# A gated linear attention with a two-layer MLP: the gate's linear half folded into one matrix, and every engine's order from a list scheduler

## The chip, the cores and the metric

The kernel runs on one core of one Trainium2 chip. A core has the engines PE (TensorE, matrix products), DVE (VectorE), ACT (ScalarE), POOL (GpSimd) and SP (SyncE, which here only issues transfers). Each takes its instructions in the order of its own list and waits where an instruction needs another engine's or a transfer's result. Stated times are device microseconds of a whole execution; the profile's span runs from its first to its last instruction.

## The reference

```python
def _attn_ref(q, k, v, f_logit):            # (4, 8, 768, 48) each
    f = 1.0 / (1.0 + np.exp(-f_logit))
    for t in range(S):
        state = f[:, :, t, :, None] * state + np.einsum('bhd,bhe->bhde', k[:, :, t], v[:, :, t])
        y[:, :, t] = np.einsum('bhd,bhde->bhe', q[:, :, t], state)

def _moe_ref(x, w_in, w_out):               # x (3072, 384), w_in (384, 2048), w_out (2048, 384)
    h = x @ w_in
    g = 0.5 * (h + np.sqrt(h * h + 4.0))
    return g @ w_out
```

The result of the attention, with its heads side by side, is the x of the MLP.

## The kernel before

The 3072 tokens are 24 chunks r of 128 (six for each of four batches); two neighbours are a pair p, and there are 12 pairs. A pair goes through these steps, which are also the functions of the code:

- `load` puts f, q, k, v of the pair into buffers, two transfers of 192 KB for each, all issued by SP. `load_w_in` and `load_w_out` load the weights in four pieces of 768 KB each, cast to fp16 by ACT (L118) and DVE (L124).
- `logs` forms the negative logarithm of the forget gate: exponential and logarithm on ACT (L133, L134), a high fp16 part on DVE (L136) and the low part on POOL (L137).
- `decays` sums the logs over a chunk on PE (L145, L146), takes two exponentials of each chunk's sums on ACT (L151, L152), multiplies q and k with them on POOL (L153, L154), and gets the boundary sums by 32 matmuls of two columns (L163, L164). `gammas` makes the factors between chunks (POOL L179, ACT L182).
- `st_T` to `st_YT` are the attention of one chunk: transposed q and k (PE and DVE, or from chunk `XBAR_FROM` = 12 on a transposing transfer), scores (L211) and their mask (DVE L213), state (L222, L225, DVE L228), y (L239, L241, DVE L244), and y transposed into `xT`.
- `mlp1` is the first layer: a half is six matmuls of 256 columns (L296) into one of four PSUM banks `hps`; for each two banks ACT squares them (L303, 512 wide) and takes the root (L304), and DVE adds half of h (L307), which gives `g16`. The decays use the same four banks.
- `mlp2` is the second layer: 16 matmuls of 384 columns for each chunk (L325), a copy (L329) and the transfer out.

ACT needs one table for exponentials and logarithms and another for roots; a load of a table is a row of ACT. So exponentials come in windows: eight `GROUPS` of chunks, and `window` runs the decays of one group and the logs of the next between two table loads. The order is written out by hand: `run_mlp1` mixes first-layer halves with attention steps from the list `att` (in the proportion `SHARE`) and second-layer quarters from the list `fill`; ACT takes its instructions exactly as written, and the other engines' orders come from the tile framework.

Of the kernel before, what the change touches and what calls it, by code (L numbers as in the profile page):

```python
# [15 lines left out]
XBAR_FROM = 12  # L16
# [3 lines left out]
GROUPS = [(0, 2), (2, 4), (4, 6), (6, 8), (8, 12), (12, 16), (16, 20), (20, 24)]  # L20
SHARE = 0.8
# [3 lines left out]
def kernel(  # L25
# [20 lines left out]
    PR = 2  # L46
    TB = PR * C

    ctx.enter_context(tc.manual_schedule(engines={mybir.EngineType.Activation}))
# [3 lines left out]
    gp = ctx.enter_context(tc.tile_pool(name="gp", bufs=4))  # L53
    stp = ctx.enter_context(tc.tile_pool(name="stp", bufs=2))
    wp = ctx.enter_context(tc.tile_pool(name="wp", bufs=2))
    bp = ctx.enter_context(tc.tile_pool(name="bp", bufs=2))
    xp = ctx.enter_context(tc.tile_pool(name="xp", bufs=5))
    mp = ctx.enter_context(tc.tile_pool(name="mp", bufs=2))
    pp_h = ctx.enter_context(tc.tile_pool(name="pp_h", bufs=1, space=PSUM))
# [15 lines left out]
    nc.vector.memset(hvec[64:128, 1:2], 1.0)  # L75

    w_in16 = konst.tile([128, NJ, DFF], FP16, name="w_in16")
    w_out16 = konst.tile([128, NN, DM], FP16, name="w_out16")

# [4 lines left out]
    qt = [t[:, :, 0] for t in qk]  # L84
    kt = [t[:, :, 1] for t in qk]
# [6 lines left out]
    for t in gam:  # L92
        nc.vector.memset(t, 0.0)
    for t in qt + kt:
        nc.gpsimd.memset(t[:, :, :, D:64], 0.0)

    hps = [pp_h.tile([128, 512], FP32, name=f"hps{i}") for i in range(4)]


    loads = {}  # L100

    def load(p, names):
        for name in names:
            src = {"f": f_logit, "q": q, "k": k, "v": v}[name]
            t = ldp.tile([128, PR, H, D], FP32, name=f"ld_{name}", tag=f"ld_{name}")
            loads[name, p] = t
            for r in range(PR):
                b, c = divmod(p * PR + r, NC)
                nc.sync.dma_start(out=t[:, r],  # L109
                                  in_=src[b][:, c * C:(c + 1) * C, :].rearrange("h t d -> t h d"))  # L110

    WQ = 512

    def load_w_in(i):
        st = stp.tile([128, 4 * DM], FP32, name="w_st", tag="w_st")
        s3 = st.rearrange("p (j n) -> p j n", j=NJ)
        nc.sync.dma_start(out=s3, in_=moe_w_in[:, i * WQ:(i + 1) * WQ].rearrange("(j p) n -> p j n", p=128))
        nc.scalar.copy(out=w_in16[:, :, i * WQ:(i + 1) * WQ], in_=s3)  # L118

    def load_w_out(i):  # L120
        st = stp.tile([128, 4 * DM], FP32, name="w_st", tag="w_st")
        s3 = st.rearrange("p (j n) -> p j n", j=4)
        nc.sync.dma_start(out=s3, in_=moe_w_out[i * 512:(i + 1) * 512, :].rearrange("(j p) n -> p j n", p=128))
        nc.vector.tensor_copy(out=w_out16[:, 4 * i:4 * i + 4, :], in_=s3)  # L124


    v16s = {}

    def logs(p):

        f = loads["f", p]
        ls = wp.tile([128, PR, H, D], FP32, name="ls", tag="ls")
        nc.scalar.activation(out=f, in_=f, func=AF.Exp, scale=-1.0)  # L133
        nc.scalar.activation(out=ls, in_=f, func=AF.Ln, bias=1.0, scale=1.0)  # L134
        hi, lo = lhi[p % NL], llo[p % NL]
        nc.vector.tensor_copy(out=hi[:, :, :, 0:D], in_=ls)  # L136
        nc.gpsimd.tensor_tensor(out=lo[:, :, :, 0:D], in0=ls, in1=hi[:, :, :, 0:D], op=ALU.subtract)  # L137

    def decays(p):

        hi, lo = lhi[p % NL], llo[p % NL]
        hp2 = [hps[2 * (p % 2) + r] for r in range(PR)]
        for r in range(PR):
            ca = hp2[r][:, 0:H * D]
            nc.tensor.matmul(out=ca, lhsT=wcent, rhs=hi[:, r, :, 0:D], start=True, stop=False)  # L145
            nc.tensor.matmul(out=ca, lhsT=wcent, rhs=lo[:, r, :, 0:D], start=False, stop=True)  # L146
        ea = wp.tile([128, PR, H, D], FP32, name="ea", tag="ea")
        eap = wp.tile([128, PR, H, D], FP32, name="eap", tag="eap")
        for r in range(PR):
            ca = hp2[r][:, 0:H * D]  # L150
            nc.scalar.activation(out=ea[:, r].rearrange("p h d -> p (h d)"), in_=ca, func=AF.Exp, scale=-1.0)  # L151
            nc.scalar.activation(out=eap[:, r].rearrange("p h d -> p (h d)"), in_=ca, func=AF.Exp, scale=1.0)  # L152
        nc.gpsimd.tensor_tensor(out=qt[p % NB][:, :, :, 0:D], in0=loads["q", p], in1=ea, op=ALU.mult)  # L153
        nc.gpsimd.tensor_tensor(out=kt[p % NB][:, :, :, 0:D], in0=loads["k", p], in1=eap, op=ALU.mult)  # L154
        v16 = bp.tile([128, PR, H, D], FP16, name="v16", tag="v16", bufs=4)
        nc.vector.tensor_copy(out=v16, in_=loads["v", p])
        v16s[p] = v16
        b, c = divmod(p * PR, NC)
        for r in range(PR):
            nl = hp2[r][:, H * D:H * D + 2 * NP].rearrange("p (j s) -> p j s", s=2)  # L160
            for hp in range(NP):
                o = nl[:, hp, :]
                nc.tensor.matmul(out=o, lhsT=hi[:, r, 2 * hp:2 * hp + 2, :], rhs=hvec, start=True, stop=False)  # L163
                nc.tensor.matmul(out=o, lhsT=lo[:, r, 2 * hp:2 * hp + 2, :], rhs=hvec, start=False, stop=True)  # L164
            nc.vector.tensor_copy(out=nls[b % 2][:, c + r], in_=nl)

    def gammas(g):
        r0, r1 = GROUPS[g]
        a = r0
        while a < r1:  # L170
            b, c = divmod(a, NC)
            e = min(r1, (b + 1) * NC)
            n = e - a
            nb, gm = nls[b % 2], gam[b % 2]
            c0 = max(c - 1, 0)
            c1 = c + n - 1
            if c1 > c0:
                gi = wp.tile([128, NC, NP], FP32, name="gi", tag="gi")
                nc.gpsimd.tensor_tensor(out=gi[:, c0:c1], in0=nb[:, c0:c1, :, 1],  # L179
                                        in1=nb[:, c0 + 1:c1 + 1, :, 0], op=ALU.add)  # L180
                for s in range(2):
                    nc.scalar.activation(out=gm[64 * s:64 * s + 64, c0:c1, :, s],  # L182
                                         in_=gi[64 * s:64 * s + 64, c0:c1], func=AF.Exp, scale=-1.0)
            a = e


    state = {}
    xTs = {}
    part = {}

    def st_T(r):
        p, i = divmod(r, PR)
        qkT = bp.tile([128, 2 * NP, C], FP16, name="qkT", tag="qkT", bufs=3)
        if r < XBAR_FROM:
            tr = pp_a.tile([128, 2 * NP, C], FP16, name="tr", tag="a")
            for j in range(NP):
                nc.tensor.transpose(out=tr[:, j, :], in_=qt[p % NB][:, i, 2 * j:2 * j + 2, :], identity=ident16)
                nc.tensor.transpose(out=tr[:, NP + j, :], in_=kt[p % NB][:, i, 2 * j:2 * j + 2, :], identity=ident16)  # L198
            nc.vector.tensor_copy(out=qkT, in_=tr)  # L199
        else:  # L200
            nc.sync.dma_start_transpose(out=qkT, in_=qk[p % NB][:, i].rearrange("p a h d -> p (a h d)"))
        part[r] = {"qkT": qkT}

    def st_SC(r):
        qkT = part[r]["qkT"]
        pm = bp.tile([128, 2, NP, C], FP16, name="pm", tag="pm")
        for s in range(2):
            sc = pp_a.tile([128, NP, C], FP32, name="sc", tag="a")
            o = 64 * s
            for j in range(NP):  # L210
                nc.tensor.matmul(out=sc[:, j, :], lhsT=qkT[o:o + D, NP + j, :], rhs=qkT[o:o + D, j, :],  # L211
                                 start=True, stop=True)
            nc.vector.tensor_tensor(out=pm[:, s], in0=sc, in1=mask16.unsqueeze(1).broadcast_to([128, NP, C]),  # L213
                                    op=ALU.mult)
        part[r]["pm"] = pm

    def st_KV(r):
        p, i = divmod(r, PR)
        b, c = divmod(r, NC)
        u = pp_a.tile([128, NP, 2, D], FP32, name="u", tag="a")  # L220
        if c > 0:
            nc.tensor.matmul(out=u.rearrange("p a b d -> p (a b d)"), lhsT=ident16,  # L222
                             rhs=state[r].rearrange("p a b d -> p (a b d)"), start=True, stop=False)
        for j in range(NP):
            nc.tensor.matmul(out=u[:, j], lhsT=kt[p % NB][:, i, 2 * j:2 * j + 2, :],  # L225
                             rhs=v16s[p][:, i, 2 * j:2 * j + 2, :], start=(c == 0), stop=(c == 0 or j == NP - 1))
# [20 lines left out]
    def st_YT(r):  # L247
        p, i = divmod(r, PR)
        if i == 0:
            xTs[p] = xp.tile([128, NJ, TB], FP16, name="xT", tag="xT")  # L250
# [226 lines left out]
```

## Time and profile before

| | us |
|---|---|
| median of 3 runs | 257.18 |
| lowest, highest | 255.63, 257.59 |
| profiled execution, whole time | 257.61 |
| its span | 255.8 |
| DVE combine L307, 96 rows, busy | 62.1 |
| ACT squares L303 and roots L304, busy | 54.1 and 50.7 |
| POOL low part L137, busy | 19.8 |
| SP waiting to issue an output, in total | 37.7 |

"Busy" of PE counts pipelined matmuls with modelled ends, so their rows overlap: 576 matmuls with a mean of 296 ns are 84.4 us busy. The granted clock is given as a share of full speed. A waiting engine's row names what came last. Groups and timelines name a line, an engine, an operation, the tile written and those read, and a count.

### The profile page before, as it was taken

How to read it: one execution, taken by the hardware profiler on the slowest of the kernel's cores; microseconds unless marked ns; L12 is line 12 of the kernel's file. 1: busy time of each engine (PE TensorE's matmuls, PEld its weight loads, DVE VectorE, ACT ScalarE, POOL GpSimd, SP SyncE). 2: the span in 40 equal slices, each digit the busy share in tenths (PEclk: the TensorE clock that was granted, in tenths of full speed). 3: DMA queues.
4: the chain of work that ended last, by engine and by line, in shares of the span. 5: the costliest groups of instructions: out<-in, count | busy, mean ns of one | idle time of the engine just before them, and what ended most of it. 6: DMA issues, size and time to landing. Idle time of an engine off the chain costs nothing.

```text
span 255.8 us, 4975 instructions
## 1 busy us (share of the span) xinstructions
PE 209.0 (82%) x1892; PEld 147.2 (58%) x1892; DVE 165.0 (64%) x303; ACT 168.1 (66%) x252; POOL 70.8 (28%) x61
## 2 busy tenths in 40 slices
PE   0337893999778799599849997799995899999994
PEld 0125672775456566466537754577764577777652
DVE  2435763885887855668954746949980779956411
ACT  3332749888588197758688995149991889987200
POOL 4447101002762209701960039300029000000000
PEclk9999997799988799769998999569999599999999
DMA  8999399999935999999979932544115320120121
GB/s 140 188 193 279 105 232 247 255 252 187 205 64 115 190 210 168 199 224 175 147 161 187 172 99 44 133 95 62 32 49 97 64 37 18 47 80 31 61 93 63
DMA packets 124696, 34.54 MB, mean 135 GB/s; under 512 B 118016, under 2 KB 123136, under 8 KB 124672
## 3 DMA queue, kind: packets, MB, share of 16 engines
q1 hardware_dynamic: 124672, 34.22, 70.4%
q8 instruction: 15, 0.25, 0.4%
q14 instruction: 9, 0.07, 0.1%
HBM read 25.17 MB, written 4.72 MB: 117 GB/s over the span
## 4 chain that ended last, share of the span: by engine, by line
PE 40%; ACT 15%; issue 13%; POOL 12%; DVE 8%; DMA 5%; SPq 3%; POOLq 1%; ACTq 0%; DVEq 0%
PE hps L296 18%; PE o L325 14%; POOL qk L154 4%; POOL qk L153 4%; ACT hsq L303 4%; ACT r L304 3%; SPq L109 3%; DVE g L307 3%; PE sc L211 3%; DMA w_st<-in_moe_w_in_dram 3%; POOL llo L137 2%; DMA ld_f<-in_f_logit_dram 2%; DVE pm L213 2%; ACT eap L152 1%; ACT w_in L118 1%
## 5 line engine op out<-in xcount | busy, mean ns | idle before, releaser
L296 PE MATMUL hps<-xT,w_in 128*128 128x256 f16 x576 | 84.4, 296 | 9.4 <-DVE g L307 8.3
L325 PE MATMUL o<-w_out,g 128*128 128x384 f16 x384 | 79.2, 333 | 0.0
L307 DVE SCALAR_TENSOR_TENSOR g<-hps,r 128x512 f16<-128x512 f32 x96 | 62.1, 685 | 24.6 <-ACT r L304 24.2
L296 PEld LDWEIGHTS <-w_in 128*128 128x128 f16 x576 | 59.0, 105 | 26.2 <-issue 12.4
L303 ACT ACTIVATE hsq<-hps 128x512 f16<-128x512 f32 x96 | 54.1, 589 | 27.3 <-PE hps L296 25.7
L304 ACT ACTIVATE r<-hsq 128x1024 f16<-128x1024 f16 x48 | 50.7, 1057 | 1.5
L153 POOL TENSOR_TENSOR qk<-ld_q,ea 128x768 f16<-128x768 f32 x12 | 22.2, 1853 | 102.3 <-ACT ea L151 60.3
L325 PEld LDWEIGHTS <-g 128*128 128x128 f16 x384 | 35.6, 99 | 19.3 <-issue 1.2
L213 DVE TENSOR_TENSOR pm<-sc,mask 128x512 f16<-128x512 f32 x48 | 31.7, 683 | 6.2 <-PE sc L211 5.8
L211 PE MATMUL sc<-qkT 48*128 48x128 f16 x192 | 19.6, 243 | 9.3 <-DVE sn L228 4.4
L137 POOL TENSOR_TENSOR llo<-ls,lhi 128x768 f16<-128x768 f32 x12 | 19.8, 1657 | 24.2 <-DVE lhi L136 24.1
L154 POOL TENSOR_TENSOR qk<-ld_k,eap 128x768 f16<-128x768 f32 x12 | 23.3, 1938 | 0.0
L211 PEld LDWEIGHTS <-qkT 48*128 48x128 f16 x192 | 11.3, 103 | 17.8 <-issue 11.1
L329 DVE COPY o_sb<-o 128x384 f32<-128x384 f32 x24 | 13.2, 552 | 13.0 <-PE o L325 13.0
L182 ACT ACTIVATE gam<-gi 64x4 f32<-64x4 f32 (+3 forms) x18 | 3.8, 208 | 24.0 <-POOL gi L179 23.9
L151 ACT ACTIVATE ea<-hps 128x384 f32<-128x384 f32 x24 | 12.1, 506 | 8.3 <-PE hps L146 8.3
L228 DVE TENSOR_TENSOR sn<-u,gam 128x384 f16<-128x384 f32 x20 | 11.1, 553 | 10.0 <-ACT gam L182 7.6
L145 PE MATMUL hps<-lhi,wcent 128*128 128x384 f16 x24 | 8.1, 355 | 9.4 <-DVE wcent L70 9.2
L199 DVE COPY qkT<-tr 128x1024 f16<-128x1024 f16 x12 | 8.3, 691 | 10.8 <-PE tr L198 10.8
L241 PE MATMUL y<-v,pm 128*128 128x48 f16 x192 | 14.4, 200 | 1.0 <-DVE qkT L199 0.8
L136 DVE CAST lhi<-ls 128x768 f16<-128x768 f32 x12 | 10.6, 890 | 6.8 <-ACT ls L134 6.8
L244 DVE CAST y<-y 128x384 f16<-128x384 f32 x24 | 13.2, 549 | 2.3 <-PE y L241 2.3
(50 smaller groups left out, 222.6 us busy)
## 6 DMA issues: line engine op xcount, KB each, us to landing
ld_f<-in_f_logit_dram SPq DMA_DIRECT2D x24, 192.0 KB, 4.6
ld_q<-in_q_dram SPq DMA_DIRECT2D x24, 192.0 KB, 4.5
ld_k<-in_k_dram SPq DMA_DIRECT2D x24, 192.0 KB, 4.6
ld_v<-in_v_dram SPq DMA_DIRECT2D x24, 192.0 KB, 4.7
out_dram<-o_sb SPq DMA_DIRECT2D x24, 192.0 KB, 1.9
w_st<-in_moe_w_in_dram SPq DMA_DIRECT2D x4, 768.0 KB, 6.7
w_st<-in_moe_w_out_dram SPq DMA_DIRECT2D x4, 768.0 KB, 5.5
qkT<-qk SPq DMA_TRANSPOSE x12, 3.3
```

The costliest lines, as they stand in the source:

```text
L137: nc.gpsimd.tensor_tensor(out=lo[:, :, :, 0:D], in0=ls, in1=hi[:, :, :, 0:D], op=ALU.subtract)
L153: nc.gpsimd.tensor_tensor(out=qt[p % NB][:, :, :, 0:D], in0=loads["q", p], in1=ea, op=ALU.mult)
L154: nc.gpsimd.tensor_tensor(out=kt[p % NB][:, :, :, 0:D], in0=loads["k", p], in1=eap, op=ALU.mult)
L211: nc.tensor.matmul(out=sc[:, j, :], lhsT=qkT[o:o + D, NP + j, :], rhs=qkT[o:o + D, j, :], start=True, stop=True)
L213: nc.vector.tensor_tensor(out=pm[:, s], in0=sc, in1=mask16.unsqueeze(1).broadcast_to([128, NP, C]), op=ALU.mult)
L241: nc.tensor.matmul(out=y[:, j, s], lhsT=pm[:, s, j, :], rhs=v16s[p][:, i, 2 * j + s, :], start=(c == 0), stop=(c == 0 or s == 1))
L244: nc.vector.tensor_copy(out=y16.rearrange("p a b -> p (a b)"), in_=y.rearrange("p a b d -> p (a b d)"))
L296: nc.tensor.matmul(out=hb[:, a, :], lhsT=w_in16[:, j, jn * 128:(jn + 1) * 128], rhs=x[:, j, :], start=(j == 0), stop=(j == NJ - 1))
L303: nc.scalar.activation(out=hsq[:, a, :], in_=hps[(2 * j4 + a) % 4], func=AF.Square, scale=1.0)
L304: nc.scalar.activation(out=r16, in_=hsq, func=AF.Sqrt, scale=0.25, bias=1.0)
L307: nc.vector.scalar_tensor_tensor(out=g16[:, jn:jn + 2, :].rearrange("p a t -> p (a t)"), in0=hps[(2 * j4 + a) % 4], scalar=0.5, in1=r16[:, ...
L325: nc.tensor.matmul(out=o, lhsT=gts[p][:, jn, i * C:(i + 1) * C], rhs=w_out16[:, jn, :], start=(jn == 0), stop=(jn == NN - 1))
```

## The change

Since 0.5 (h + sqrt(h² + 4)) w_out = 0.5 x w_in w_out + sqrt(0.25 h² + 1) w_out, the linear part is x times one 384x384 matrix. `add_transposed_w_in` transposes the fp16 w_in on PE (48 transposes), `add_linear_part` multiplies it with w_out (48 matmuls) and stores half of it as `w_lin`. In the second layer each chunk then starts with three matmuls of `xT` with `w_lin`. The DVE combine is gone; the root writes `g16` itself.

The instructions are also cut differently. A first-layer tile is 1024 wide, with two such tiles of two banks in a ring; a square is 1024 wide and a root 2048; an exponential of the decays covers both chunks (768). The low part of the logs goes from POOL to DVE, the sum of the gammas too. Weights come in sixteen pieces of 384 KB through the rings of q, k and v, and DVE casts all of them. Chunks 10 and 11 are transposed by transfers too.

Every step is first put down as an `Op` with engine, assumed duration, dependencies, buffers and a due time. `Plan.run` then places them one by one: for each engine the head of each queue that could start first, within 0.05 us the one with the earliest due time, with rules that keep an exponential window of ACT together. The instructions are written out in this order for all engines.

```diff
-GROUPS = [(0, 2), (2, 4), (4, 6), (6, 8), (8, 12), (12, 16), (16, 20), (20, 24)]
+GROUPS = [[0], [1], [2], [3], [4, 5], [6, 7], [8, 9], [10, 11]]
-XBAR_FROM = 12
+XBAR_FROM = 10
+PACE = 15.5
+LEAD = {"W": 45.0, "B": 26.0, "M1": 0.0, "M2": -30.0}
...
+    def run(self):
...
+                t0 = min(c[0] for c in cands)
+                near = [c for c in cands if c[0] <= t0 + 0.05]
+                c = min(near, key=lambda c: c[1].due)
+                if best is None or c[0] < best[0]:
+                    best = c + (eng,)
...
-    ctx.enter_context(tc.manual_schedule(engines={mybir.EngineType.Activation}))
+    ctx.enter_context(tc.manual_schedule())
...
-        nc.gpsimd.tensor_tensor(out=lo[:, :, :, 0:D], in0=ls, in1=hi[:, :, :, 0:D], op=ALU.subtract)
+            nc.vector.tensor_tensor(out=llo[p % NL][:, :, :, 0:D], in0=T["ls", p],
+                                    in1=lhi[p % NL][:, :, :, 0:D], op=ALU.subtract)
...
+                nc.scalar.activation(out=t.rearrange("p r h d -> p r (h d)"), in_=T["ca", p][:, :, 0:H * D],
+                                     func=AF.Exp, scale=sign)
...
+    def add_transposed_w_in():
...
+                        for j in range(NJ):
+                            nc.tensor.transpose(out=t[:, b, j * 128:(j + 1) * 128],
+                                                in_=w_in16[:, j, jn * 128:(jn + 1) * 128], identity=ident16)
...
+                    nc.vector.tensor_copy(out=wiT[n][:, 2 * a:2 * a + 2, :], in_=T["wtp", n, a])
...
+    def add_linear_part(t_ops):
...
+                    for jn in range(4 * n, 4 * n + 4):
+                        nc.tensor.matmul(out=T["wl", j], lhsT=wiT[jn // 8][:, jn % 8, j * 128:(j + 1) * 128],
+                                         rhs=w_out16[:, jn, :], start=(jn == 0), stop=(jn == NN - 1))
...
+                nc.vector.tensor_scalar(out=w_lin[:, j, :], in0=T["wl", j], scalar1=0.5, scalar2=None, op0=ALU.mult)
...
-                nc.scalar.activation(out=hsq[:, a, :], in_=hps[(2 * j4 + a) % 4], func=AF.Square, scale=1.0)
-            nc.scalar.activation(out=r16, in_=hsq, func=AF.Sqrt, scale=0.25, bias=1.0)
-                nc.vector.scalar_tensor_tensor(out=g16[:, jn:jn + 2, :].rearrange("p a t -> p (a t)"),
-                                               in0=hps[(2 * j4 + a) % 4], scalar=0.5, in1=r16[:, a, :],
-                                               op0=ALU.mult, op1=ALU.add)
+                nc.scalar.activation(out=T["hsq", p, j8][:, j4 % 2],
+                                     in_=T["h", p, j4].rearrange("p a n -> p (a n)"), func=AF.Square, scale=1.0)
...
+                nc.scalar.activation(out=T["g", p][:, 8 * j8:8 * j8 + 8, :].rearrange("p a t -> p (a t)"),
+                                     in_=T["hsq", p, j8].rearrange("p a n -> p (a n)"), func=AF.Sqrt, scale=0.25, bias=1.0)
...
+                        for j in range(NJ):
+                            nc.tensor.matmul(out=T["o", p, i], lhsT=T["xT", p][:, j, i * C:(i + 1) * C],
+                                             rhs=w_lin[:, j, :], start=(j == 0), stop=False)
+                    for jn in range(4 * n, 4 * n + 4):
+                        nc.tensor.matmul(out=T["o", p, i], lhsT=T["g", p][:, jn, i * C:(i + 1) * C],
+                                         rhs=w_out16[:, jn, :], start=False, stop=(jn == NN - 1))
...
+    P.run()
+    for op in P.order:
+        if op == "exp":
+            nc.scalar.preload_act_table_set("natural_log_exp_and_others")
+        elif op == "sqrt":
+            nc.scalar.preload_act_table_set("sqrt_and_others")
         else:
+            op.emit()
```

The loads are written in this order: f, q, k, v of pairs 0 and 1; the eight pieces of w_in, with f of pair 2 after the fourth; the eight of w_out; q, k, v of pair 2; then f, q, k, v of each pair. SP's list before, from the ninth row on (w_st is the buffer for a piece of weights, the other names are the buffers of pair 2 and then pair 3):

```order
L117 DMA w_st<-in_moe_w_in_dram 128x3x512 x2
L109 DMA ld_f<-in_f_logit_dram 128x8x48 x2
L117 DMA w_st<-in_moe_w_in_dram 128x3x512 x2
L109 DMA ld_q<-in_q_dram 128x8x48 x2
L109 DMA ld_k<-in_k_dram 128x8x48 x2
L109 DMA ld_v<-in_v_dram 128x8x48 x2
L123 DMA w_st<-in_moe_w_out_dram 128x4x384 x2
L109 DMA ld_f<-in_f_logit_dram 128x8x48
```

SP's list after, at the end of the weights (the last three pieces of w_out, then pair 2 and f of pair 3):

```order
L287 DMA ld_v<-in_moe_w_out_dram 128x2x384
L287 DMA ld_q<-in_moe_w_out_dram 128x2x384
L287 DMA ld_k<-in_moe_w_out_dram 128x2x384
L266 DMA ld_q<-in_q_dram 128x8x48 x2
L266 DMA ld_k<-in_k_dram 128x8x48 x2
L266 DMA ld_v<-in_v_dram 128x8x48 x2
L266 DMA ld_f<-in_f_logit_dram 128x8x48 x2
```

All sixteen pieces of weights now stand ahead of q, k and v of pair 2. Before, half of w_in stood behind f of pair 2 and w_out behind the whole of pair 2.

ACT before, at the window with the decays of pair 2 and the logs of pair 3 (ea and eap are the two exponentials, ld_f and ls the logs, gam the gammas):

```order
L304 ACTIVATE r_705<-hsq 128x1024
L369 ACT_TABLE_LOAD
L151 ACTIVATE ea<-hps_143 128x384
L152 ACTIVATE eap<-hps_143 128x384
L151 ACTIVATE ea<-hps_144 128x384
L152 ACTIVATE eap<-hps_144 128x384
L133 ACTIVATE ld_f<-ld_f 128x768
L134 ACTIVATE ls<-ld_f 128x768
L182 ACTIVATE gam_121<-gi 64x8 x2
L382 ACT_TABLE_LOAD
```

ACT after, at the same window:

```order
L668 ACTIVATE g_429<-hsq 128x2048
L742 ACT_TABLE_LOAD
L365 ACTIVATE ea<-hps 128x768
L365 ACTIVATE eap<-hps 128x768
L318 ACTIVATE ld_f<-ld_f 128x768
L323 ACTIVATE ls<-ld_f 128x768
L416 ACTIVATE gi<-gi 128x8
L660 ACTIVATE hsq<-hps 128x1024 x2
L744 ACT_TABLE_LOAD
```

Before, both pairs 0 and 1 have gone through the first layer ahead of this window; after, only pair 0 has, and the squares of pair 1 stand behind the logs of pair 3, still ahead of the next table load.

More of the change, by code (lines that the diff above doesn't have):

```diff
@@ L91, with ring, add_load, emit @@
         nc.vector.memset(t[:, :, :, D:64], 0.0)
[L92 to L106, printed above, removed]
+    for t in qk:
+        nc.gpsimd.memset(t[:, :, :, :, D:64], 0.0)
+    P = Plan()
+    T = {}
+    rings = {}
+    def ring(name, n):
+        return rings.setdefault(name, Ring(n))
+    ld = {}
+    ld_buf = {}
+    src_of = {"f": f_logit, "q": q, "k": k, "v": v}
+    LB = {"f": 3, "q": 4, "k": 4, "v": 4}
+    def add_load(p, name):
+        buf = Buf(ring("ld_" + name, LB[name]))
+        ld_buf[name, p] = buf
+        def emit():
+            t = ldp.tile([128, PR, H, D], FP32, name=f"ld_{name}", tag=f"ld_{name}", bufs=LB[name])
+            T[name, p] = t
             for r in range(PR):
@@ L127 @@
[L127 to L157, printed above, removed]
-        b, c = divmod(p * PR, NC)
[L159 to L165, printed above, removed]
@@ L172, in gammas @@
             e = min(r1, (b + 1) * NC)
[L173 to L183, printed above, removed]
@@ L184, in gammas @@
-            a = e
[L187 to L215, printed above, removed]
@@ L218, in st_KV, with add_attention @@
+            o2 = P.add("W", "ACT", 0.25, ex, deps=[o1], due=due, uses=[gi_b], kind=("W", g))
+            o3 = P.add("gam", "DVE", 0.2, spread, deps=[o2], due=due, uses=[gi_b])
+            for cc in range(c0, c1):
+                gm[b * NC + cc] = o3
+    state_op = {}
+    xT_ops = {}
+    def add_attention(r):
         p, i = divmod(r, PR)
         b, c = divmod(r, NC)
-        u = pp_a.tile([128, NP, 2, D], FP32, name="u", tag="a")
-        if c > 0:
-            nc.tensor.matmul(out=u.rearrange("p a b d -> p (a b d)"), lhsT=ident16,
-                             rhs=state[r].rearrange("p a b d -> p (a b d)"), start=True, stop=False)
@@ L224, in st_KV @@
[L224 to L232 removed]
+        due = vtime(p, "B", i * PACE / 2)
@@ new lines, in add_attention, with yf @@
+        a_b = Buf(ring("a", 2))
+        def yf():
+            y = pp_a.tile([128, NP, 2, D], FP32, name="y", tag="a")
+            T["y", r] = y
+            for j in range(NP):
+                if c > 0:
+                    nc.tensor.matmul(out=y[:, j], lhsT=T["qkT", r][:, j, :], rhs=T["sn", r][:, j], start=True, stop=False)
+                for s in range(2):
+                    nc.tensor.matmul(out=y[:, j, s], lhsT=T["pm", r][:, s, j, :], rhs=T["v16", p][:, i, 2 * j + s, :],
+                                     start=(c == 0), stop=(c == 0 or s == 1))
@@ L233, in st_Y, with add_state @@
+        xT_ops.setdefault(p, []).append(op)
+    def add_state(r, due):
         p, i = divmod(r, PR)
         b, c = divmod(r, NC)
-        qkT, pm = part[r]["qkT"], part[r]["pm"]
-        y = pp_a.tile([128, NP, 2, D], FP32, name="y", tag="a")
-        for j in range(NP):
-            if c > 0:
-                nc.tensor.matmul(out=y[:, j], lhsT=qkT[:, j, :], rhs=state[r][:, j], start=True, stop=False)
-            for s in range(2):
-                nc.tensor.matmul(out=y[:, j, s], lhsT=pm[:, s, j, :], rhs=v16s[p][:, i, 2 * j + s, :],
-                                 start=(c == 0), stop=(c == 0 or s == 1))
@@ new lines @@
+    for n in "fqkv":
+        add_load(0, n)
+    for n in "fqkv":
+        add_load(1, n)
+    for i in range(8):
+        add_weight("in", i)
+        if i == 3:
+            add_load(2, "f")
+    for i in range(8):
+        add_weight("out", i)
+    for n in "qkv":
+        add_load(2, n)
+    for p in range(3, NPAIR):
+        for n in "fqkv":
+            add_load(p, n)
+    NG = len(GROUPS)
+    for p in GROUPS[0]:
+        add_logs(p, 0)
+    for g in range(NG):
+        for p in GROUPS[g]:
+            add_decays(p, g)
+        if g + 1 < NG:
+            for p in GROUPS[g + 1]:
+                add_logs(p, g)
+        add_gammas(g)
```

638 lines of the change are left out of this document (435 added, 203 removed).

## The prediction

> **What bounds the kernel now.** I read the page first (busy shares, slices, chain of waits), then the stretches between the start and the last matmul, then the groups by line, and last the timelines of single engines for durations. Page, one line of each part:
>
> ```profile
> span 255.8 us, 4975 instructions
> ...
> PE 209.0 (82%) x1892; PEld 147.2 (58%) x1892; DVE 165.0 (64%) x303; ACT 168.1 (66%) x252; POOL 70.8 (28%) x61
> ...
> PE   0337893999778799599849997799995899999994
> ...
> PEclk9999997799988799769998999569999599999999
> ...
> PE 40%; ACT 15%; issue 13%; POOL 12%; DVE 8%; DMA 5%; SPq 3%; POOLq 1%; ACTq 0%; DVEq 0%
> ```
>
> PE leads the shares and the chain, but it has holes, and the granted clock falls in six places. The stretches (duration; then busy us and count for PE, PEld, DVE, ACT, POOL; granted clock; DMA share; GB/s) say how much that is:
>
> ```profile
> 42.70:252.50 209.80, 188.34 (x1694) 132.59 (x1693) 144.31 (x254) 147.77 (x224) 54.92 (x36) 0.91 0.66 125
> 158.00:160.00 2.00, 1.07 (x16) 0.76 (x16) 2.00 (x6) 0.71 (x3) 2.00 (x3) 1.00 0.73 139
> 162.00:164.00 2.00, 1.63 (x13) 1.01 (x12) 1.93 (x4) 0.00 (x0) 0.42 (x1) 0.50 0.57 111
> ```
>
> A busy PE is not a PE at its peak, so I work out what its work costs in dense rows, start to start. Chain of waits, then the PE timeline:
>
> ```profile
> 148.44 1.28 ACT L369
> ...
> 233.01 0.66 PE hps L296 x6
> 233.66 0.65 PE o L325 x4
> ...
> 236.28 16.26 PE o L325 x100
> 252.56 0.56 DVE o_sb L329
> ```
>
> ```profile
> 35.80 0.33 PE L255 MATMUL yt<-ident,y 128*128 128x128 f16 x3
> 35.96 0.49 PE L296 MATMUL hps<-xT,w_in 128*128 128x256 f16 x3
> 36.29 0.21 PE L239 MATMUL y<-sn,qkT 128*128 128x96 f16 x1
> ...
> 36.66 0.93 PE L296 MATMUL hps<-xT,w_in 128*128 128x256 f16 x7
> ...
> 58.76 0.33 PE L145 MATMUL hps<-lhi,wcent 128*128 128x384 f16 x1
> ...
> 59.41 2.44 PE L325 MATMUL o<-w_out,g 128*128 128x384 f16 x14
> ```
>
> ```profile
> 171.62 0.45 PE L211 MATMUL sc<-qkT 48*128 48x128 f16 x8
> 171.99 2.23 PE L296 MATMUL hps<-xT,w_in 128*128 128x256 f16 x18
> 174.05 0.33 PE L222 MATMUL u<-sn,ident 128*128 128x384 f16 x1
> ...
> 174.39 0.33 PE L325 MATMUL o<-w_out,g 128*128 128x384 f16 x1
> ...
> 190.18 0.16 PE L163 MATMUL hps<-hvec,lhi 128*128 128x2 f16 x1
> ...
> 190.38 0.32 PE L325 MATMUL o<-w_out,g 128*128 128x384 f16 x1
> ```
>
> Dense prices: 0.109 us for a first-layer matmul (0.65 for 6), 0.163 for a second-layer one (16.26 for 100). For one chunk of 128 tokens: y transposed 0.16, y 0.37, scores 0.37, state 0.34, q/k transposed 0.43 (eight 128-wide transposes at the 0.16 for three). One pair's decays 0.65 + 2 x 0.20 = 1.05. So the whole kernel is 576 x 0.109 + 384 x 0.163 + 24 x (0.37 + 0.37) + 20 x 0.34 + 12 x (0.43 + 0.16) + 12 x 1.05 = 62.8 + 62.6 + 17.8 + 6.8 + 7.1 + 12.6 = 169.7 us of PE at full speed. By 42.7 us some 11.4 of it is done (4 chunks, 2 decays, 24 first-layer matmuls); the other 158.3 take 209.8, a loss of 51.5. The clock accounts for 0.09 x 209.8 = 19 of that, plain idle time for 209.8 - 188.3 = 21.5, the rest sits inside rows called busy. What empties PE (groups, waits):
>
> ```profile
> L296 PE MATMUL hps<-xT,w_in 128*128 128x256 f16 x576 | 84.4, 296 | 9.4 <-DVE g L307 8.3 <-DMA xT<-y 0.6
> L307 DVE SCALAR_TENSOR_TENSOR g<-hps,r 128x512 f16<-128x512 f32 x96 | 62.1, 685 | 24.6 <-ACT r L304 24.2
> L303 ACT ACTIVATE hsq<-hps 128x512 f16<-128x512 f32 x96 | 54.1, 589 | 27.3 <-PE hps L296 25.7 <-DVE qkT L199 0.9
> L304 ACT ACTIVATE r<-hsq 128x1024 f16<-128x1024 f16 x48 | 50.7, 1057 | 1.5
> L137 POOL TENSOR_TENSOR llo<-ls,lhi 128x768 f16<-128x768 f32 x12 | 19.8, 1657 | 24.2 <-DVE lhi L136 24.1
> L133 ACT ACTIVATE ld_f<-ld_f 128x768 f32<-128x768 f32 x12 | 10.2, 852 | 3.1 <-DMA ld_f<-in_f_logit_dram 3.1
> L151 ACT ACTIVATE ea<-hps 128x384 f32<-128x384 f32 x24 | 12.1, 506 | 8.3 <-PE hps L146 8.3
> ```
>
> A PSUM bank of the first layer passes through matmul, square, root and the DVE combine before it is free, and in ACT's exponential windows nothing consumes those banks at all.
>
> **The change, part by part.** *Linear half folded.* PE gains 72 matmuls of 384 columns (3 per chunk) = 11.7 us, and once 48 transposes (2.6) and 48 matmuls (7.8) for the folded matrix. Two chunks fewer are transposed on PE (12 to 10): -1.2. PE work becomes 190.6. DVE loses 62.1 and gains 8 copies and 3 scalings at about 0.55 (6 us) and the casts of w_in that ACT did (some 4); all of these lie in the start. The bank is free after the square: the part from square end to combine end (root 1.06 and two combines, 1.3) goes, so the wait of 8.3 on L307 goes with it; what is late next is ACT itself, a 1024-wide square plus half a root.
>
> *Wider ACT instructions.* A square of 1024 costs between 0.59 (no price for width) and 1.18 (twice the 512 row), near the upper, 1.05; a root of 2048 between 1.06 and 2.11, I take 1.9; an exponential of 768 between 0.51 and 1.01, 0.83 as L133. Behind the point named below ACT has 44 squares, 22 roots, 18 exponentials, 16 at 0.85 and 11 table loads of 1.28: 46 + 42 + 15 + 14 + 14 = 131 us, against 164 for PE. PE stays the bound; the upper ends would make 145, still below.
>
> *Low part from POOL to DVE.* Between 0.56 (a DVE cast of this size) and 1.66 (POOL's row); a 768-wide DVE operation with the pace of the 512-wide one at 0.69 is 0.95. Twelve are 11 us on a DVE that has lost 62. It shortens the way from a load of f to its decays by some 0.7.
>
> *Start, queue of SP.* All sixteen weight pieces now stand ahead of q, k, v of pair 2 and f of pair 3, and behind f of pair 3 ACT holds the first layer of pair 1, and PE (through the decays of pair 3) all the rest. Up to that f there are 13 loads and 16 pieces of 0.393 MB each, 11.4 MB. What the queue moved in stretches without the hole at 25 to 30 us, and what lies between a landed f and its decays:
>
> ```profile
> 0.00:25.00 25.00, 9.07 (x87) 5.91 (x88) 9.66 (x30) 8.34 (x15) 12.61 (x23) 1.00 1.16 204
> 30.00:55.00 25.00, 19.92 (x157) 14.60 (x156) 16.38 (x27) 19.06 (x25) 1.64 (x1) 0.86 0.99 259
> ```
>
> ```profile
> 5.10 0.84 ACT L133 ACTIVATE ld_f<-ld_f 128x768 f32<-128x768 f32 x1 [3.09 <-DMA ld_f<-in_f_logit_dram]
> ```
>
> ```profile
> 9.23 0.82 PE L145 MATMUL hps<-lhi,wcent 128*128 128x384 f16 x2 [9.23 <-DVE wcent L70]
> ```
>
> 5.1 MB in 25 us and 6.3 MB at 259 GB/s in 24.3: f of pair 3 lands near 50. The way to the decays was 9.23 - 5.10 = 4.1, less some 0.5 now: 53.6. By then PE has done 54 first-layer matmuls, 3 decays, 4 chunks and a transpose, and the folded matrix: 26.7 us, all under the loads. Behind 53.6 lie 190.6 - 26.7 = 163.9.
>
> *The order of all engines.* What remains is what the new order loses. Bounds: nothing (the run of 100 above is seamless), or the old rate, 51.5 over six windows = 8.6 each. There are five exponential windows behind 53.6. A window of two pairs holds ACT for 1.28 + 4 x 0.83 + 4 x 0.85 + a small one, about 8.5, until the next square; between the first decays of such a window and the next full first-layer tile the new PE order has 19 second-layer matmuls, half a tile, two decays, two y, two states, two half scores and two transposes: 3.1 + 0.65 + 2.1 + 0.74 + 0.68 + 0.37 + 0.32 = 8.0. So 0.5 bare, plus the hand-offs of the attention chain, which in the window of before read
>
> ```profile
> 158.06 0.33 PE L225 MATMUL u<-v,qk 128*128 128x96 f16 x4 [0.90 <-DVE pm L213]
> 158.66 0.36 PE L241 MATMUL y<-v,pm 128*128 128x48 f16 x8 [0.27 <-DVE pm L213]
> ...
> 160.05 0.38 PE L211 MATMUL sc<-qkT 48*128 48x128 f16 x4 [0.55 <-DVE y L244]
> 160.65 0.43 PE L222 MATMUL u<-sn,ident 128*128 128x384 f16 x1 [0.22 <-DVE pm L213]
> ```
>
> 1.9 in four gaps: 2.5 a window, 12.5 in all, nearer the lower bound because second-layer work lies between the links now. One drop of the clock (before: 19 over six, 3.1 each) I add for the start of the dense part.
>
> These gaps are under a microsecond, PE was busy 1.07 of 2.00 us, and yet the clock stood at 0.50 from 162 on: sparse work lost the clock here, not silence. The Trainium skill (TensorE: Matmul & The Clock Gate, Part 1) says that the clock halves after an idle window of about 3.4 us and returns after a busy one. Read as silence, no gap of 2.5 would cost clock, and the sum would be 3.1 lower, about 235. The trace does not bear that reading out, so the term stays.
>
> Sum: 53.6 + 163.9 + 12.5 + 3.1 + 3.3 (last matmul at 252.5 to the span's end) = 236.4. The profiled execution took 257.61 for a span of 255.8, and the median of the runs shown is 257.18, so 1.8 on top: 238.
>
> **Rivals.** *The windows stay as they were* (slower). The new order is fixed on every engine, so one late instruction in a window holds all behind it. At 8.6 for each of five windows the sum is 53.6 + 163.9 + 43 + 3.3 + 1.8 = 266. It decides from 6.3 a window on. For it: PE has more work and ACT's windows are as long. Against: the freed banks, and cover of 8.0.
>
> *The loads come late* (weights in 1 KB rows at the 204 GB/s of the first stretch): 6.3 MB take 30.8 instead of 24.3, the point moves by 6.5, 245. For it: everything hangs on one queue. Against: 259 was reached with mixed loads.
>
> *Nearly seamless*: a loss of 3 behind the point, 226. For it: 207 to 252 us of before, dense with DVE and ACT at work. Against: no exponential window lies there.
>
> *The fold without effect* is excluded: the combine is gone from the program. ACT as the bound gives less than 164, so it is none.
>
> **How the numbers follow.** 0.56 for the forecast (230 to 243), 0.15 seamless, 0.13 late loads, 0.06 for windows near 6.3 (about 257), 0.10 for 266. Eight in ten: from 225 (seamless) to 255, which leaves out the last two cases. A measurement of this kernel can tell about 1% from no change; faster by more 0.84, within 0.06, slower 0.10.
>
> **What would show it.** f of pair 3 lands at 50 and PE is without a hole over 3 us behind 55; no wait of PE for DVE at the first layer; ACT near 156 us busy (48 x 1.05 + 24 x 1.9 + 24 x 0.83 + 24 x 0.85 + 14 x 1.28 + 2), DVE near 123 (165 - 62 + 6 + 4 + 11, rounded); squares of 1024 at 1.05, roots of 2048 at 1.9; the clock over 0.95 behind 60. Wrong if PE's holes in the five windows exceed 6 us each, if the first layer waits for squares all along (ACT bounds), or if the pieces of weights land after 48.

## The result and the profile after

| | before | after |
|---|---|---|
| median of 4 runs each, us | 256.77 | 242.27 |
| lowest, highest | 255.63, 257.59 | 241.53, 243.28 |
| ratio, 95% interval | | 0.944 [0.939, 0.950] |
| profiled execution: whole time, span | 257.61, 255.8 | 242.64, 240.9 |

The forecast was 238 with a range of 225 to 255. Ratios, here and below, leave out executions in a second, slower state of the chip, and times from different experiments are compared by these ratios, 1% being 2.6 us. The page of the kernel after, the same lines as before:

```profile
span 240.9 us, 4922 instructions
...
PE 209.4 (87%) x2038; PEld 151.1 (63%) x2038; DVE 134.4 (56%) x243; ACT 149.2 (62%) x143; POOL 47.6 (20%) x36
...
PE   0372698799999994999599999999999999999994
...
PEclk9997587799999999799999999999999999999998
...
PE 74%; DVE 12%; ACT 3%; issue 3%; DMA 3%; POOL 2%; SPq 1%; POOLq 0%; ACTq 0%
```

PE's share of the chain went from 40% to 74%. From the thirteenth slice up to the last but one PE has two thin slices and the clock one; before it had thin slices up to the thirty-first. Its own groups and ACT's (count, busy us, mean ns, idle time ahead of them):

```profile
L652 PE MATMUL hps<-xT,w_in 128*128 128x256 f16 x576 | 75.5, 279 | 5.2 <-ACT hsq L660 4.2
...
L660 ACT ACTIVATE hsq<-hps 128x1024 f16<-128x1024 f32 x48 | 48.3, 1018 | 36.1 <-PE hps L652 35.6
...
L668 ACT ACTIVATE g<-hsq 128x2048 f16<-128x2048 f16 x24 | 45.8, 1910 | 0.6
```

The first layer no longer waits for DVE's combine, and ACT's squares now wait for PE 35.6 us in all: the bound is PE. Three stretches of the kernel after (duration; busy us and count of PE, PEld, DVE, ACT, POOL; clock; DMA share; GB/s), up to the folded matrix (all but six of its transposes), up to the decays of pair 3, and up to the end of the last matmul:

```profile
0.00:45.00 45.00, 24.20 (x245) 17.91 (x246) 34.99 (x66) 18.85 (x21) 10.58 (x16) 0.85 0.98 249
45.00:58.65 13.65, 13.46 (x112) 9.89 (x112) 9.52 (x21) 4.37 (x6) 3.59 (x2) 0.87 1.05 208
58.65:237.30 178.65, 171.75 (x1684) 123.26 (x1681) 89.34 (x157) 126.01 (x117) 33.42 (x18) 0.99 0.56 118
```

Ahead of 45 us PE is idle for 20.8, behind 58.65 for 6.9 of 178.65. What it does between the two, and ACT's side of the load that the prediction hung the start on:

```profile
45.05 3.69 PE L598 MATMUL wtp<-ident,w_in 128*128 128x128 f16 x30 [0.40 <-DVE wiT L604]
48.58 0.81 PE L621 MATMUL wl<-w_out,wiT 128*128 128x384 f16 x4
...
50.72 6.66 PE L621 MATMUL wl<-w_out,wiT 128*128 128x384 f16 x40
...
58.65 0.33 PE L352 MATMUL hps<-lhi,wcent 128*128 128x384 f16 x1
```

```profile
46.80 0.80 ACT L365 ACTIVATE eap<-hps 128x768 f32<-128x768 f32 x1
47.49 0.84 ACT L318 ACTIVATE ld_f<-ld_f 128x768 f32<-128x768 f32 x1
```

f of pair 3 was there when ACT came to it at 47.5: that row has no wait. The decays of pair 3 stand behind the folded matrix in PE's list, and PE, 99% busy from 45.0 on, reaches them only at 58.65. DVE's list has the same order: the high and low part of pair 3's logs stand behind the second scaling of the folded matrix, for which DVE waits, although ACT's logarithm was done at 49.2.

```profile
54.82 0.56 DVE L627 TENSOR_SCALAR w_lin<-wl 128x384 f16<-128x384 f32 x1 [1.76 <-PE wl L621]
55.29 0.55 DVE L326 CAST lhi<-ls 128x768 f16<-128x768 f32 x1
...
55.88 0.96 DVE L329 TENSOR_TENSOR llo<-ls,lhi 128x768 f16<-128x768 f32 x1
```

So these decays could not have begun before 56.8 in this order, wherever PE had stood.

### The profile page after: what moved, and what is told of

It is laid out like the page before. It is cut to its first block, busy times and chain, and to the rows that moved or that the text cites. A ratio compares the mean times of both kernels' runs of the same rounds, so it can differ in the third digit from the quotient of the medians.

```text
span 240.9 us, 4922 instructions
## 1 busy us (share of the span) xinstructions
PE 209.4 (87%) x2038; PEld 151.1 (63%) x2038; DVE 134.4 (56%) x243; ACT 149.2 (62%) x143; POOL 47.6 (20%) x36
## 4 chain that ended last, share of the span: by engine, by line
PE 74%; DVE 12%; ACT 3%; issue 3%; DMA 3%; POOL 2%; SPq 1%; POOLq 0%; ACTq 0%
PE o L686 25%; PE hps L652 24%; PE o L683 5%; PE sc L488 4%; PE wl L621 3%; DVE pm L494 2%; PE tr L464 2%; DVE lhi L326 2%; PE y L511 2%; POOL qk L371 2%; DMA ld_q<-in_q_dram 2%; DVE v L377 1%; PE hps L352 1%; DVE w_in L294 1%; PE wtp L598 1%
## 5 line engine op out<-in xcount | busy, mean ns | idle before, releaser
L652 PE MATMUL hps<-xT,w_in 128*128 128x256 f16 x576 | 75.5, 279 | 5.2 <-ACT hsq L660 4.2
L686 PE MATMUL o<-w_out,g 128*128 128x384 f16 x384 | 73.9, 326 | 0.0
L660 ACT ACTIVATE hsq<-hps 128x1024 f16<-128x1024 f32 x48 | 48.3, 1018 | 36.1 <-PE hps L652 35.6
L686 PEld LDWEIGHTS <-g 128*128 128x128 f16 x384 | 35.8, 98 | 20.5
L668 ACT ACTIVATE g<-hsq 128x2048 f16<-128x2048 f16 x24 | 45.8, 1910 | 0.6
L365 ACT ACTIVATE ea<-hps 128x768 f32<-128x768 f32 x12 | 9.7, 811 | 27.2 <-PE hps L359 27.2
L488 PE MATMUL sc<-qkT 48*128 48x128 f16 x192 | 15.5, 227 | 2.7 <-DVE xT L547 1.4
L683 PE MATMUL o<-w_lin,xT 128*128 128x384 f16 x72 | 15.9, 330 | 0.0
L318 ACT ACTIVATE ld_f<-ld_f 128x768 f32<-128x768 f32 x12 | 10.1, 838 | 8.8 <-DMA ld_f<-in_f_logit_dram 8.8
L511 PE MATMUL y<-v,pm 128*128 128x48 f16 x192 | 11.7, 185 | 1.1 <-DVE pm L494 1.1
L464 PE MATMUL tr<-ident,qk 128*128 128x128 f16 x80 | 7.7, 257 | 5.6 <-POOL qk L371 4.1
L511 PEld LDWEIGHTS <-pm 128*128 128x128 f16 x192 | 10.0, 98 | 3.1 <-issue 2.0
```

What stands on the lines that cost most here:

```text
L488: nc.tensor.matmul(out=t[:, j, :], lhsT=qkT[o:o + D, NP + j, :], rhs=qkT[o:o + D, j, :], start=True, stop=True)
L511: nc.tensor.matmul(out=y[:, j, s], lhsT=T["pm", r][:, s, j, :], rhs=T["v16", p][:, i, 2 * j + s, :], start=(c == 0), stop=(c == 0 or s == 1))
L652: nc.tensor.matmul(out=hb[:, a, :], lhsT=w_in16[:, j, jn * 128:(jn + 1) * 128], rhs=T["xT", p][:, j, :], start=(j == 0), stop=(j == NJ - 1))
L660: nc.scalar.activation(out=T["hsq", p, j8][:, j4 % 2], in_=T["h", p, j4].rearrange("p a n -> p (a n)"), func=AF.Square, scale=1.0)
L668: nc.scalar.activation(out=T["g", p][:, 8 * j8:8 * j8 + 8, :].rearrange("p a t -> p (a t)"), in_=T["hsq", p, j8].rearrange("p a n -> p (a ...
L683: nc.tensor.matmul(out=T["o", p, i], lhsT=T["xT", p][:, j, i * C:(i + 1) * C], rhs=w_lin[:, j, :], start=(j == 0), stop=False)
```

## Experiments

Two theories: (A) PE's work and its start set the time, so what counts is how full the order keeps PE; (B) the fold brings the gain, because it frees tiles and takes the combine from DVE. Ratios are to the kernel before, run on the same chip in the same job.

**The fold alone.** The kernel before, with its own order:

```diff
-            nc.scalar.activation(out=r16, in_=hsq, func=AF.Sqrt, scale=0.25, bias=1.0)
-            for a in range(2):
-                nc.vector.scalar_tensor_tensor(...)
+            nc.scalar.activation(out=g16[:, 4 * j4:4 * j4 + 4, :].rearrange("p a t -> p (a t)"),
+                                 in_=hsq.rearrange("p a n -> p (a n)"), func=AF.Sqrt, scale=0.25, bias=1.0)
...
+    transposed_w_in()
     run_mlp1(0, 1)
+    fill[0:0] = linear_part()
```

> The kernel before with the fold alone: its order by hand, its sizes and its queues stay; the DVE combine goes, the root writes g, 48 transposes and 48 matmuls form the matrix while pair 1 is in the first layer, and each chunk has three more matmuls. Theory A (the new order brings the gain; the fold in itself adds 22 us to PE and takes away one wait of 8.3 and what DVE held up): between 252 and 262. Theory B (the fold brings the gain, by freeing the banks after the square): 247 or less, with PE's idle time behind 43 us well under the 21.5 of before.

Measured: ratio 1.011 [1.005, 1.018], near 259. A, on this side. The first layer's wait for the combine is gone, but in the profiled execution (263.3 us, one of the longer ones) PE is still idle for 18.1 us behind 43 us, where it was 21.5 before; the hand-written windows are as they were:

```profile
43.00:258.00 215.00, 196.91 (x1802) 136.95 (x1801) 91.64 (x162) 145.55 (x224) 54.95 (x36) 0.94 0.64 123
```

So in the old order the fold costs some 3 us. Most of its 22 us of PE work finds room in time that PE lost before, but only 3.4 us of it is plain idle time; where the rest found room is not shown.

**The order alone**, and a control for the four dependencies that it needed. "Order" stands here for all of the change but the fold: the 1024-wide squares, the weights in sixteen pieces and the low part on DVE are in it too, and these were not tried apart:

```diff
+                nc.vector.scalar_tensor_tensor(out=T["g", p][:, 4 * j4:4 * j4 + 4, :].rearrange("p a t -> p (a t)"),
+                                               in0=T["h", p, j4].rearrange("p a n -> p (a n)"), scalar=0.5,
+                                               in1=T["r", p, j4], op0=ALU.mult, op1=ALU.add)
...
-    t_ops = add_transposed_w_in()
-    add_linear_part(t_ops)
```

> The changed kernel without the fold: the list scheduler, the loads, the 1024-wide squares and the low part on DVE stay; a root is 1024 wide and a DVE combine per 1024 columns holds the tile until it is done; no folded matrix, no linear matmuls. Transposes by transfers begin with chunk 12 as before, and four dependencies within the attention keep the scheduler from running into its own buffers. Theory A (PE's work and its start set the time): 22 us less on PE than the changed kernel, so 222 to 232. Theory B (without the freed banks PE waits again): 245 or more.

> Control for the run of the order alone: the changed kernel, fold and all, with the same four dependencies in the attention and transposes by transfers from chunk 12. If these cost nothing, 240 to 245 like the changed kernel, and the time of the order alone (244.4 with 21 us less on PE) is due to the missing fold. If they are what slowed it, 248 or more here.

Measured: 244.42, ratio 0.951 [0.945, 0.957]; the control 240.87, 0.939 [0.932, 0.946], so the dependencies cost nothing. Theory B in its plain form falls here, since 4.9 of the 5.6% come without the fold. So does theory A: with 21 us less on PE the order alone is no faster than the changed kernel. DVE is busy for 187.6 us (77%), and PE has holes in two stretches of the order alone:

```profile
70.00:100.00 30.00, 21.47 (x199) 15.13 (x197) 22.66 (x34) 17.89 (x20) 7.17 (x4) 0.83 1.01 212
100.00:130.00 30.00, 26.89 (x287) 19.52 (x286) 26.64 (x39) 22.32 (x25) 7.77 (x4) 0.94 0.71 142
```

PE is idle for 8.5 and 3.1 us in them at a clock of 0.83 and 0.94; DVE is at 89% in the second. To part DVE's load from the hold on the tiles, the combine was cut to 8 columns; it still holds the tile behind the root, but the second layer now reads what the root writes:

```diff
-                nc.vector.scalar_tensor_tensor(...)
+                t = sp.tile([128, 8], FP16, name="r16", tag="r16", bufs=2)
+                nc.vector.scalar_tensor_tensor(out=t, in0=T["h", p, j4][:, 0, 0:8], scalar=0.5,
+                                               in1=T["r", p, j4][:, 0:8], op0=ALU.mult, op1=ALU.add)
```

> The order alone, in its own order, with a combine of 8 columns in place of 1024 (the root writes g, and the output lacks the linear half). A tile is still held until a DVE instruction behind the root has read it, so the chain matmul, square, root, combine stays; DVE's share of it falls from 1.22 us to some 0.2, 48 x 1.0 = 49 us in all. If the load on DVE is what the fold takes away (DVE was 77% busy in the order alone), 10 or more go from 244.4: 222 to 234, near the changed kernel less its 21 us. If the hold on the tile is what counts, at most 5 go: 239 to 245. If the gaps are the order's own, as planned, it stays within 2 of 244.

Measured: 234.84, ratio 0.920 [0.914, 0.926] against 0.951: 3.1% or 8 us, just short of the 10 expected for DVE's load. PE's waits for the combine tell the same, first with the full one, then with the narrow one (in total, times, longest):

```profile
PE hps L652 <- DVE g L669: 3.9, 6, 1.4
PE hps L351 <- DVE g L669: 2.6, 2, 1.6
PE o L688 <- DVE g L669: 2.4, 2, 1.2
```

```profile
PE hps L351 <- DVE r L670: 0.6, 1, 0.6
...
PE hps L652 <- DVE r L670: 0.4, 1, 0.4
```

8.9 us become 1.0. The changed kernel less the fold's 21 us of PE work would be at 221 (an estimate from the dense prices), and the order alone is 23 above that; DVE's time is 8 of these 23. For the other 15 the hold on the tiles, which still lasts until the root, shows as a wait of PE of only the 1.0. PE's idle time is 39.9 us with the narrow combine and 31.5 in the changed kernel, and the waits left are mostly gaps of that one order: 4.15 us at 90 us for a state on DVE, 4.16 in the run with the full combine, and 4.09 ahead of the decays at 49 us. What the scheduler gave up because it knew of the longer hold was not tried.

**How much of the fold's PE work is paid.** The linear matmuls left out, and the forming of the matrix left out, both in the changed kernel's own order:

```diff
-                        for j in range(NJ):
-                            nc.tensor.matmul(out=T["o", p, i], lhsT=T["xT", p][:, j, i * C:(i + 1) * C],
-                                             rhs=w_lin[:, j, :], start=(j == 0), stop=False)
```

> The changed kernel in its own order, with the 72 matmuls of x with the folded matrix left out (the output then lacks the linear half). If PE sets the time from 45 us on, all of their 72 x 0.163 = 11.7 us go: 230 to 232. If hand-offs with ACT and DVE set it, PE waits in their place and less than 5 go.

Measured: ratio 0.894 [0.888, 0.901], near 230: 5.0% or 12.8 us less than the changed kernel, for 11.7 us of matmuls. In the profile some 12.2 of it lie behind the decays of pair 3 (166.4 us up to the end of the last matmul, for 178.65), and these decays came 1.2 us earlier, at 57.46, with nothing taken out ahead of them but a granted clock of 1.00 all along. So in this order all of these matmuls' time counts.

```diff
     for op in P.order:
...
-            op.emit()
+            if op not in prep:
+                op.emit()
```

> The changed kernel in its own order, with the forming of the folded matrix left out (48 transposes, 48 matmuls, 8 copies, 3 scalings; the matrix is a constant, so the output's linear half is not the reference's). In the profile it runs on PE from 45.0 to 57.2 us, while f of pair 3 was there at 47.5. If it is what made the start 5 us later than predicted, 5 to 8 us go: 234 to 237. If the loads or DVE's casts set the start, at most 2 go. If all its PE time is on the path, 11 go.

Measured: 238.07, ratio 0.926 [0.922, 0.931]: 1.8% or 4.6 us less, between the cases. The profile tells why it isn't more (decays of pair 3; the stretch of 45 to 58.65; from the decays to the last matmul):

```profile
50.88 0.52 PE L352 MATMUL hps<-lhi,wcent 128*128 128x384 f16 x1
```

```profile
45.00:58.65 13.65, 10.73 (x77) 6.59 (x78) 7.40 (x14) 4.98 (x7) 3.85 (x2) 0.55 1.09 216
50.90:232.70 181.80, 174.44 (x1683) 124.61 (x1681) 90.91 (x160) 126.00 (x117) 33.40 (x18) 0.97 0.60 126
```

The point moves from 58.65 to 50.88, 7.8 us, and 3.2 of these are given back: 181.8 instead of 178.65 lie behind it. The clock accounts for that: it stands at 0.58 from the point to 58.65, which is 3.3 of 7.8 us lost. With the matrix the low clock came earlier (0.85 ahead of 45 us, where this run has 0.99). That the missing matmuls moved it is not shown: from 20 to 25 us PE is busy 1.04 us in both, and the clock is 0.62 with the matrix and 1.00 without. Without the matrix the load is next in line: ACT waits 1.12 us for f of pair 3, until 48.3.

**What holds the start.** DVE is 78% busy ahead of 45 us, and its casts of w_in take 0.94 us each against 0.55 for those of w_out, for as many values. One run keeps w_in16 piece by piece, one puts these casts on ACT:

```diff
-    w_in16 = konst.tile([128, NJ, DFF], FP16, name="w_in16")
+    w_in16 = konst.tile([128, 8, NJ, 256], FP16, name="w_in16")
...
-                nc.vector.tensor_copy(out=w_in16[:, :, i * 256:(i + 1) * 256], in_=st.rearrange("p (j n) -> p j n", j=NJ))
+                nc.vector.tensor_copy(out=w_in16[:, i], in_=st.rearrange("p (j n) -> p j n", j=NJ))
```

> The changed kernel in its own order; w_in16 is kept piece by piece, so that each of DVE's eight casts of w_in writes 768 values in a row as those of w_out do. In the profile the casts of w_in take 0.94 us and those of w_out 0.55. If the way the target lies is the reason, they fall to about 0.55 and DVE gets 3.1 us back between 22 and 35 us. If DVE holds the start, 1 to 3 us go: 239 to 241. If the loads or the folded matrix hold it, under 1 goes.

```diff
-                nc.vector.tensor_copy(out=w_in16[:, :, i * 256:(i + 1) * 256], in_=...)
+                nc.scalar.copy(out=w_in16[:, :, i * 256:(i + 1) * 256], in_=...)
```

> The changed kernel in its own order, with the eight casts of w_in on ACT in place of DVE, each at the place that the order gives it. DVE loses 7.5 us between 22 and 35 us, where it is 86% busy; ACT waits there. If DVE holds the start, more goes than with the faster casts: 237 to 240. If not, 241 to 243. If ACT's table loads or its squares are held up by a cast that waits for its transfer, 243 or more.

Measured: casts in rows 241.04, 0.939 [0.934, 0.944]; casts on ACT 243.45, 0.948 [0.942, 0.954], beside 0.944 [0.939, 0.950] for the changed kernel. The casts in rows did fall to 0.55:

```profile
L294 DVE CAST w_in<-ld_q 128x768 f16<-128x768 f32 x3 | 1.6, 548 | 0.0
```

and in the profile the decays of pair 3 came at 56.6, 2 us earlier, with 178.7 behind them as ever. The clock stood at 1.00 up to there, as in the run without the linear matmuls, where they came at 57.46; so of the 2 us some 0.9 are left for the casts. In the time it is 0.5% or 1.4 us, and the intervals overlap: at most a little. On ACT the first layer of pair 0 began 1.6 us earlier (27.8 for 29.4), and PE then waited 2.2 for a square behind the casts. DVE's casts hold at most a small part of the start.

**Another order.** The casts in rows with other due times:

```diff
-PACE = 15.5
-LEAD = {"W": 45.0, "B": 26.0, "M1": 0.0, "M2": -30.0}
+PACE = 16.0
+LEAD = {"W": 35.0, "B": 26.0, "M1": 0.0, "M2": -30.0}
```

> The casts in rows of the run above and another order: PACE 16 in place of 15.5, and a lead of 35 in place of 45 for the decays and logs, so that first and second layer go ahead of them more often. If the windows of ACT are what is left behind 58 us (7.1 us of PE idle time there), later decays can only shift them: within 2 of the casts in rows. If the early decays push first-layer work aside, 3 or more go: 235 to 238.

Measured: 240.48, 0.939 [0.933, 0.945]: no difference from the casts in rows. This one other order neither won nor lost.

**Less work on PE.** If A holds in the changed kernel, work must come off PE. The low fp16 part of the logs is left out: the sums over a chunk then take the high part alone, which rounds the logs to fp16.

```diff
-                nc.tensor.matmul(out=ca, lhsT=wcent, rhs=lhi[p % NL][:, r, :, 0:D], start=True, stop=False)
-                nc.tensor.matmul(out=ca, lhsT=wcent, rhs=llo[p % NL][:, r, :, 0:D], start=False, stop=True)
+                nc.tensor.matmul(out=ca, lhsT=wcent, rhs=lhi[p % NL][:, r, :, 0:D], start=True, stop=True)
```

> The casts in rows, in the order of the changed kernel, and in the decays the low fp16 part of the logs is left out: the sums over a chunk use the high part alone (a rounding of the logs to fp16). PE loses 24 matmuls of 384 columns (3.9 us) and 96 of two columns (2.4 us), DVE 12 subtractions (11 us). If PE's work sets the time from 45 us on, 4 of these 6.3 us go for certain (the decays of the first three pairs lie ahead of it) and up to 6: 235 to 237. If the exponential windows set it, the decays at their start shorten them only by DVE's subtraction once for each: 239 to 241.

> The same, with the scheduler told of the shorter decays and the missing subtraction, PACE 15.75 in place of 15.5 and a lead of 22 in place of 26 for the attention. If PE's work is what counts, the new order can take away only what is left of idle time behind the start (7.1 us in the changed kernel): 230 to 236. If the order itself matters little, as the run with other due times showed, it ends within 2 of the run with the order kept.

Measured: 233.03, ratio 0.911 [0.906, 0.916], and 232.34, 0.908 [0.902, 0.915] with the order planned anew: 2.8% or 7 us under the casts in rows, where 4 to 6 were expected, and nothing clear more from the plan. The first of them, from the decays of pair 3 to the last matmul:

```profile
55.10:227.10 172.00, 167.12 (x1595) 119.91 (x1592) 82.74 (x149) 125.87 (x117) 33.31 (x18) 0.99 0.60 126
```

Behind the point 6.7 went (178.7 to 172.0) for 4.8 us of matmuls of nine pairs (9 x 0.53), so PE's idle time fell too, from 6.9 to 4.9. What went are waits for DVE, which had 11 us less to do: for its y from 1.2 to 0.3 us, for its state from 0.7 to nothing; the wait for ACT's squares stayed at 3.5. The point itself came 1.5 earlier. These two are the fastest of the kernels here that leave out no term of the formula, at the price of the rounded logs.

## Why the prediction was right, point by point

*The bound and the direction.* PE with its holes was the bound, and the change closed them: idle and slow-clock time behind the start went from 21.5 and 19 us of 209.8 to 6.9 and 2 of 178.65. Right; that PE is the bound behind the start is shown by the linear matmuls, whose 11.7 us cost some 12. That the order of the instructions closed the holes, and not the wider ACT instructions or the other loads that came with it, is argued and not shown.

*The start.* The mis-sized term: 53.6 predicted for the decays of pair 3, 58.65 measured. The load came in time (by 47.5, predicted 50). Wrong was "26.7 us, all under the loads": the folded matrix was taken for hidden, but PE comes to all but six of its transposes only at 45.05, at a clock of 0.51 up to 48, and ends it at 57.2. Left out, it gives 7.8 us at that point and 4.6 in the time. About 1.2 of the 5.05 us read as the clock: the run without the linear matmuls, with the matrix and at full clock, has the point at 57.46.

*Behind the start.* 163.9 + 12.5 + 3.1 = 179.5 predicted, 178.65 measured. The total is right, the parts are not: idle time is 6.9 and not 12.5, the clock lost 1 to 2 us and not 3.1 there, and some 6 us lie inside rows called busy, by which the dense prices were 3 to 4% low. These errors cancel, so that the total agrees to 1 us is luck. The prediction put the drop of the clock at the start of the dense part; it lies ahead of it (0.85 and 0.87 in the first two stretches). It is not the same in every execution: the mean clock of the four is 0.955 to 0.990, and their times lie within 1.8 us.

*The ends.* 3.6 us from the last matmul to the span's end (3.3) and 1.7 on top (1.8). The errors are +5.05 for the point, -0.85 behind it and +0.3 at the end: 240.9 for the span instead of 236.4.

*The prices.* Square 1.02 (1.05), root 1.91 (1.9), exponential 0.81 (0.83), low part on DVE 0.96 (0.95). ACT is busy for 149 us, predicted 156; DVE for 134, predicted 123; 3.1 of the 11 more are the slow casts.

*The fold.* Of its effects the prediction named the freed bank and the DVE time taken off, and gave the first a wait of 8.3. The wait for the combine did go: PE waits 8.9 us for it in the order alone, and none in the changed kernel. But the two runs with one half of the change each show that the gain is the other half's: the fold alone is 1.1% slower, the order alone 4.9% faster, both 5.6%. Beside the new order the fold pays for its 21 us on PE and little more: 0.7% to the changed kernel, with intervals that overlap, and 1.2% to the control, with intervals that touch. The prediction had not split the gain in this way.

*The rivals.* None came: no window cost 6 us (PE's longest hole behind 55 us is 2.55, a wait for a square at 94 us), the loads were not late, ACT did not bound. What made the time longer than forecast, the matrix, was in none of them.

## What to carry to other kernels

When an order is made tight, what was hidden in holes is no longer hidden: price every instruction on the engine that will be full at its whole length, preparation too, and look in that engine's list for what stands ahead of the first instruction that the rest waits for. Moving work from a 64% busy engine to the bound one lost 1% here in the old order and won about 1% at most in the new one, where the other engine would have been 77% busy and often the one waited for; test the two halves of such a change apart. Once the engine was full, another order of the same work changed nothing, and taking work off it behind the start took at least as much off the time.

## What was not expected of the hardware

A DVE cast of 768 values took 0.94 us where its target was three runs of 256 and 0.55 where it was one run, with source, types and count the same. The Trainium skill (VectorE: DVE Perf Modes, What auto-detection actually checks) says that the two-port modes need the outermost dimensions of source and target to be even or equal. If the source, which lies in one piece, counts as one run, three against one is neither, and the two times fit that; no run here shows how the source counts.

A DVE operation of eight values took 1.56 us at 20.5 us of the kernel after, and a cast of 1.37 came just ahead of it, while POOL multiplied; the same cast takes 0.55 and the same operation 0.17 at 51 and 53 us:

```profile
19.00 1.37 DVE L377 CAST v<-ld_v 128x768 f16<-128x768 f32 x1
...
20.48 1.56 DVE L411 TENSOR_TENSOR gi<-nls 128x8 f32<-128x8 f32 x1
```

```profile
18.14 1.81 POOL L371 TENSOR_TENSOR qk<-ld_q,ea 128x768 f16<-128x768 f32 x1 [4.13 <-ACT ea L365]
19.91 2.11 POOL L371 TENSOR_TENSOR qk<-ld_k,eap 128x768 f16<-128x768 f32 x1
```

Behind them in DVE's list stood the y of chunk 0, for which PE waited 3.1 us. The cast ends 0.4 us behind POOL's first multiplication (20.37 and 19.95), the small operation with the second (22.04 and 22.02), as if each had waited for it. That POOL's work is the cause was not tested.
